# Nine loads instead of fourteen ahead of the DMA transposes of a fused dense, Mish, dense kernel

## The chip, the cores and the metric

The kernel runs on one core of one Trainium2 chip. A core has five engines with queues of their own: TensorE (PE, matmuls; its weight loads are listed apart as PEld), VectorE (DVE), ScalarE (ACT), GpSimd (POOL) and SyncE (SP). SP and ACT also issue the DMAs, each on a queue of its own; the core's 16 DMA engines carry out both queues. The metric is the time of one execution on the device in microseconds (us); the profile of one execution shows where it goes. The engines run side by side and wait for each other by semaphores only where the program says so.

## The reference

One row block `x` of 2048 x 512, two weight matrices, one bias, all bf16:

```python
B, S, D, F = 1, 2048, 512, 1792
def reference(x, w1, b1, w2):
    h = jnp.einsum("bsd,df->bsf", x, w1) + b1
    sp = jnp.log1p(jnp.exp(-jnp.abs(h))) + jnp.where(h > 0, h, jnp.zeros_like(h))
    act = h * jnp.tanh(sp)                      # Mish
    return jnp.einsum("bsf,fd->bsd", act, w2)
```

## The kernel before, in words

All of `x`, `w1` and `w2` fits into the on-chip memory, so everything is loaded once. The 2048 rows are cut into five blocks (`BLOCKS`: 256, 512, 512, 512, 256 rows). For each block, `mm1` (matmuls at line 172) computes the hidden values transposed: for each of 14 tiles f of 128 hidden columns, four matmuls (k = 0 to 3, one for each 128 of the 512 input columns) add up in one bank of PSUM. ScalarE then applies bias and Mish and writes `a_sb` in bf16 (`mish`, line 155). `mm2` (line 188) multiplies `a_sb` by `w2`: for each 128 rows, 14 matmuls of 512 columns add up in a bank, VectorE copies the result to `o_sb` (line 194), SP stores it.

`mm1` needs `x` transposed (`xT`). For blocks 1 to 4 a DMA transpose does it, issued on SP. For block 0, TensorE does it: `x_nat` holds the 256 rows as they are, `transpose_x` (line 144) transposes them through PSUM, and VectorE and ScalarE copy each half to `xT` (line 148).

The order of the work is written out by hand. Every load has a semaphore of its own (`load`, line 84), which is full only when all of the load has landed, and an instruction waits for the load that holds its operand. The loads of the start:

- on ACT's queue: the bias b1, then the k=0 rows of w1 for the first four tiles (`F0` = 4, 128 KB);
- on SP's queue: the two 128-row parts of `x_nat`; k = 1, 2, 3 of w1 for tiles 0 to 3 (128 KB each); w1 for tiles 4 to 7 in two loads (k 0 and 1, k 2 and 3, 256 KB each); w1 for tiles 8 to 13 in two (384 KB each); w2 in three (tiles 0 to 3, 4 to 8, 9 to 13: 512, 640, 640 KB); behind all of these the four DMA transposes of `x`.

TensorE's queue runs: seven dummy matmuls (`WARM`), the eight transposes of block 0, `mm1` of tiles 0 to 3 of block 0 in three passes (first 128 rows with k 0 and 1, the other 128 rows with k 0 and 1, then all 256 rows with k 2 and 3), between the second and the third of them a transpose of the bias (line 221), so that VectorE can put it into `b1_sb` (line 223) as one value per partition, which `mish` needs; then `mm1` of tiles 4 to 13 of block 0, tile after tile; `mm2` of block 0, which goes tile by tile over w2 with its two 128-row halves side by side (28 matmuls); then blocks 1 to 4, each all of `mm1` and then all of `mm2`. A PSUM bank is used again when ScalarE or VectorE has read it (`free`).

Of the kernel before, what the change touches and what calls it, by code (L numbers as in the profile page):

```python
# [4 lines left out]

P = 128
WARM = (512,) * 5 + (128,) * 2
BLOCKS = (256, 512, 512, 512, 256)


# [21 lines left out]
def bass_standalone__dense_activation_mish__prompt_kernel(  # L32
# [10 lines left out]
    BF, F32 = dt.bfloat16, dt.float32  # L43
# [3 lines left out]
    KT, FT = D // P, F // P  # L47
    assert (S, D, F) == (2048, 512, 1792) and sum(BLOCKS) == S
    x2, out2 = x[0], out[0]
# [3 lines left out]
    F0 = 4  # L53
    N0 = BLOCKS[0] // P

    with ExitStack() as es:
        def sb(name, shape, t):
            return es.enter_context(nc.sbuf_tensor(name, shape, t))

        x_nat = sb("x_nat", [P, N0, D], BF)  # L60
# [4 lines left out]
        b1_pad = sb("b1_pad", [P, P], BF)  # L65
        b1_sb = sb("b1_sb", [P, FT], F32)
        ones = sb("ones", [P, P], BF)
        ident = sb("ident", [P, P], BF)
        a_sb = sb("a_sb", [P, FT, S], BF)
        o_sb = sb("o_sb", [P, S // P, D], BF)  # L70
        ps = es.enter_context(nc.psum_tensor("ps", [P, 8, 512], F32))

        def sem(name):
            return es.enter_context(nc.semaphore(name))

        sp = Stream(nc.sync, None)
        pe = Stream(nc.tensor, sem("c_pe"))
        dve = Stream(nc.vector, sem("c_dve"))
        act = Stream(nc.scalar, sem("c_act"))
        pool = Stream(nc.gpsimd, sem("c_pool"))  # L80

        def load(q, dst, src, name, transpose=False):
            s = sem(name)
            (q.eng.dma_start_transpose if transpose else q.eng.dma_start)(dst, src).then_inc(s, 16)  # L84
            return (s, 16)

        def load_w1(q, ks, a, b):
            return load(q, w1_sb[:, ks, a * P:b * P], w1v[:, ks, a * P:b * P], "s_w1_%d_%d" % (ks.start, a))


        t_xn, t_w1 = [None] * N0, {}
        t_b1 = load(act, b1_nat[:, :], b1.rearrange("(j p) -> j p", p=P), "s_b1")
        t_xn[0] = load(sp, x_nat[:, 0, :], x2[0:P, :], "s_xn0")
        t_w1[0, 0] = load_w1(act, slice(0, 1), 0, F0)
        t_xn[1] = load(sp, x_nat[:, 1, :], x2[P:2 * P, :], "s_xn1")
        for k in range(1, KT):
            t_w1[k, 0] = load_w1(sp, slice(k, k + 1), 0, F0)
        for f in range(1, F0):
            for k in range(KT):
                t_w1[k, f] = t_w1[k, 0]  # L100
        for a, b in ((4, 8), (8, FT)):
            for ks in (slice(0, 2), slice(2, 4)):
                t = load_w1(sp, ks, a, b)
                for f in range(a, b):
                    for k in range(ks.start, ks.stop):
                        t_w1[k, f] = t
        t_w2 = {}
        for a, b in ((0, 4), (4, 9), (9, FT)):
            t = load(sp, w2_sb[:, a:b, :], w2v[:, a:b, :], "s_w2_%d" % a)
            for f in range(a, b):  # L110
                t_w2[f] = t
# [16 lines left out]
        def dummy(n):  # L128
            nc.tensor.matmul(ps[:, 7, 0:n], c_w, c_m[:, 0:n], start=True, stop=True)  # L129


        free = [[] for _ in range(8)]
# [19 lines left out]
        def mish(s, f, bank, t_mm):  # L152
            n = BLOCKS[s]
            act.wait(t_b1c, t_mm)
            t = act.mark(act.eng.activation(a_sb[:, f, starts[s]:starts[s + 1]], ps[:, bank, 0:n], ACT.Mish,  # L155
                                            bias=b1_sb[:, f:f + 1]))
            t_mish[s, f] = t
            free[bank] = [t]

        def mm1_step(s, f, k, bank, js=None):  # L160

            n = BLOCKS[s]
            lo, hi = (0, n) if js is None else (js[0] * P, (js[-1] + 1) * P)
            first = k == 0 and lo == 0
            if first:
                pe.wait(*free[bank])
            pe.wait(t_w1[k, f])
            if s:
                pe.wait(t_xT[s])
            else:  # L170
                pe.wait(*[t_cp[j, k // 2] for j in (js or range(N0))])
            return nc.tensor.matmul(ps[:, bank, lo:hi], w1_sb[:, k, f * P:(f + 1) * P],  # L172
                                    xT[:, k, starts[s] + lo:starts[s] + hi], start=first, stop=(k == KT - 1))

        def mm1(s, f, bank):
            for k in range(KT):
                mm = mm1_step(s, f, k, bank)
            mish(s, f, bank, pe.mark(mm))
# [4 lines left out]
        def mm2_step(i, f, lo, hi, bank):  # L183
            s = max(b for b in range(len(BLOCKS)) if starts[b] <= i * P)
            if f == 0:
                pe.wait(*free[bank])
            pe.wait(t_w2[f], t_mish[s, f])
            return nc.tensor.matmul(ps[:, bank, 0:hi - lo], a_sb[:, f, i * P:(i + 1) * P], w2_sb[:, f, lo:hi],  # L188
                                    start=(f == 0), stop=(f == FT - 1))
# [15 lines left out]

        for n in WARM:
            dummy(n)
        transpose_x(0)
        transpose_x(1)
        dve.wait(t_b1, t_bz)  # L210
        t_b1p = dve.mark(nc.vector.tensor_copy(b1_pad[0:FT, :], b1_nat[:, :]))  # L211
        for js, ks in (((0,), (0, 1)), ((1,), (0, 1)), ((0, 1), (2, 3))):
            for k in ks:
                for f in range(F0):
                    mm = mm1_step(0, f, k, 4 + f, js)
                    if k == KT - 1:
                        mish(0, f, 4 + f, pe.mark(mm))
            if js == (1,):
                pe.wait(t_b1p, *free[0])
                psb1 = ps[:, 0, 0:P // 2].bitcast(BF)  # L220
                t_b1t = pe.mark(nc.tensor.transpose(psb1, b1_pad[:, :], ident[:, :]))  # L221
                dve.wait(t_b1t)
                t_b1c = dve.mark(nc.vector.tensor_copy(b1_sb[:, :], psb1[:, 0:FT]))  # L223
                free[0] = [t_b1c]
        for f in range(F0, FT):
            mm1(0, f, {4: 1, 5: 2, 6: 3, 7: 0, 12: 2, 13: 3}.get(f, 4 + f % 4))
        for f in range(FT):
            for j in range(N0):
                mm = mm2_step(j, f, 0, D, j)
# [41 lines left out]
```

## Time and profile before

| what | value |
|---|---|
| time, median of 3 runs | 107.5 us (107.32 to 107.57) |
| the profiled execution | 107.65 us |
| its span, first to last instruction | 106.4 us |
| PE busy | 101.2 us (95% of the span) |
| ACT busy | 43.1 us (40%) |
| DVE busy | 12.1 us (11%) |
| loaded from HBM by plain loads / stored | 3.94 MB / 2.10 MB |

The profiled execution took 1.25 us more than its span, which lies outside of what the trace shows. A row of the timeline gives the start in us, the duration in us, the engine, the line of the kernel, the operation, what it writes and reads (the names without numbers: `w_sb` stands for both w1 and w2), the count, and in brackets how long the engine was idle before it and what ended that. SPq and ACTq are the queues of SP and ACT in which DMAs are issued: the duration there is that of the issue, not of the transfer. A row of the DMA view gives the queue, the count, the size, and the time from issue to landing. The chain of waits is followed back from the last instruction; where it names an engine, that engine worked without a break, where it names a DMA, everything waited for that DMA.

### The profile page before, as it was taken

How to read it: one execution, taken by the hardware profiler on the slowest of the kernel's cores; microseconds unless marked ns; L12 is line 12 of the kernel's file. 1: busy time of each engine (PE TensorE's matmuls, PEld its weight loads, DVE VectorE, ACT ScalarE, POOL GpSimd, SP SyncE). 2: the span in 40 equal slices, each digit the busy share in tenths (PEclk: the TensorE clock that was granted, in tenths of full speed). 3: DMA queues.
4: the chain of work that ended last, by engine and by line, in shares of the span. 5: the costliest groups of instructions: out<-in, count | busy, mean ns of one | idle time of the engine just before them, and what ended most of it. 6: DMA issues, size and time to landing. Idle time of an engine off the chain costs nothing.

```text
span 106.4 us, 1244 instructions
## 1 busy us (share of the span) xinstructions
PE 101.2 (95%) x542; PEld 51.7 (49%) x542; DVE 12.1 (11%) x22; ACT 43.1 (40%) x73; POOL 0.7 (1%) x6
## 2 busy tenths in 40 slices
PE   6957899999999999999999999999999999999993
PEld 2725754444444444444444444444444444588462
DVE  0200000400000222200000222200000222200023
ACT  2456630287772000188882000088883000199200
POOL 2000000000000000000000000000000000000000
DMA  2999999991000110110000101110000001110011
GB/s 82 259 259 312 374 244 202 208 270 66 0 0 0 49 47 8 49 49 0 0 3 0 49 12 37 55 49 0 0 0 0 28 21 49 49 55 0 0 49 49
DMA packets 13569, 7.94 MB, mean 75 GB/s; under 512 B 7932, under 2 KB 13564, under 8 KB 13564
## 3 DMA queue, kind: packets, MB, share of 16 engines
q1 hardware_dynamic: 13392, 7.74, 27.4%
q10 hardware_dynamic: 172, 0.13, 0.4%
q8 instruction: 4, 0.07, 0.3%
q14 instruction: 1, 0.01, 0.0%
HBM read 3.94 MB, written 2.10 MB: 57 GB/s over the span
## 4 chain that ended last, share of the span: by engine, by line
PE 88%; DMA 6%; SPq 3%; issue 0%; DVE 0%
PE ps L188 45%; PE ps L172 42%; DMA w_sb<-in_w_dram 6%; SPq L84 3%; DVE o_sb L194 0%
## 5 line engine op out<-in xcount | busy, mean ns | idle before, releaser
L155 ACT ACTIVATE a_sb<-ps,b_sb 128x512 bf16<-128x512 f32 (+1 forms) x70 | 41.0, 602 | 53.4 <-PE ps L172 53.4
L172 PE MATMUL ps<-xT,w_sb 128*128 128x512 bf16 (+2 forms) x288 | 50.2, 332 | 2.5 <-DMA w_sb<-in_w_dram 1.9
L188 PE MATMUL ps<-w_sb,a_sb 128*128 128x512 bf16 (+2 forms) x238 | 49.2, 366 | 0.0
L172 PEld LDWEIGHTS ps<-xT,w_sb 128*128 128x128 bf16 x288 | 27.2, 98 | 25.0 <-DMA w_sb<-in_w_dram 3.0
L188 PEld LDWEIGHTS ps<-w_sb,a_sb 128*128 128x128 bf16 x238 | 22.8, 98 | 25.5
L194 DVE CAST o_sb<-ps 128x512 bf16<-128x512 f32 (+2 forms) x17 | 11.1, 659 | 88.0 <-PE ps L188 88.0
L129 PE MATMUL ps<-const-bfloat16-1.0 128*128 128x512 bf16 (+1 forms) x7 | 2.5, 533 | 0.8 <-PEq L256 0.8
L123 ACT ACT_TABLE_LOAD x1 | 1.3, 1283 | 1.9 <-issue 1.9
L129 PEld LDWEIGHTS ps<-const-bfloat16-1.0 128*128 128x128 bf16 x7 | 0.9, 135 | 2.2 <-issue 2.2
L148 ACT ACTIVATE xT<-ps 128x256 bf16<-128x256 bf16 x2 | 0.8, 383 | 0.6 <-PE ps L144 0.6
L144 PE MATMUL ps<-ident,x_nat 128*128 128x128 bf16 x8 | 1.0, 305 | 0.0
L148 DVE COPY xT<-ps 128x256 bf16<-128x256 bf16 x2 | 0.6, 292 | 2.7 <-PE ps L144 2.6
L144 PEld LDWEIGHTS ps<-ident,x_nat 128*128 128x128 bf16 x8 | 0.9, 147 | 0.0
L223 DVE CAST b_sb<-ps 128x14 f32<-128x14 bf16 x1 | 0.2, 173 | 1.1 <-PE ps L221 1.1
L121 POOL TENSOR_SCALAR_AFFINE_SELECT ident<-ones 128x128 bf16<-128x128 bf16 x1 | 0.3, 292 | 0.1
L221 PE MATMUL ps<-ident,b_pad 128*128 128x128 bf16 x1 | 0.2, 219 | 0.0
L118 DVE MEMSET b_pad<- 128x64 uint32 x1 | 0.1, 112 | 0.9 <-PEq L256 0.9
L119 POOL MEMSET ones<- 128x128 bf16 x1 | 0.2, 204 | 0.3 <-POOLq L256 0.3
L211 DVE COPY b_pad<-b_nat 14x128 bf16<-14x128 bf16 x1 | 0.2, 172 | 0.0
L256 POOL MEMSET const-bfloat16-1.0<- 128x1 bf16 x1 | 0.1, 101 | 0.0
L256 POOL MEMSET const-uint8-127<- 128x1 uint8 x1 | 0.1, 101 | 0.0
L256 POOL MEMSET const-float32-0.0<- 128x1 f32 x1 | 0.1, 98 | 0.3 <-issue 0.3
(2 smaller groups left out, 0.2 us busy)
## 6 DMA issues: line engine op xcount, KB each, us to landing
out_dram<-o_sb SPq DMA_DIRECT2D x15, 128.0 KB, 1.7
w_sb<-in_w_dram SPq DMA_DIRECT2D x2, 640.0 KB, 9.4
w_sb<-in_w_dram SPq DMA_DIRECT2D x2, 384.0 KB, 6.3
w_sb<-in_w_dram SPq DMA_DIRECT2D x2, 256.0 KB, 4.3
w_sb<-in_w_dram SPq DMA_DIRECT2D x1, 512.0 KB, 7.5
w_sb<-in_w_dram SPq DMA_DIRECT2D x3, 128.0 KB, 2.9
x_nat<-in_x_dram SPq DMA_DIRECT2D x2, 128.0 KB, 2.0
w_sb<-in_w_dram ACTq DMA_DIRECT2D x1, 128.0 KB, 2.5
```

Source lines behind the costliest of these rows:

```text
L84: (q.eng.dma_start_transpose if transpose else q.eng.dma_start)(dst, src).then_inc(s, 16)
L119: t_ones = pool.mark(pool.eng.memset(ones[:, :], 1.0))
L121: t_id = pool.mark(pool.eng.affine_select(ident[:, :], ones[:, :], pattern=[[1, P]], compare_op=ALU.is_equal, fill=0.0, base=0, channel_mu ...
L123: act.eng.preload_act_table(ACT.Mish)
L129: nc.tensor.matmul(ps[:, 7, 0:n], c_w, c_m[:, 0:n], start=True, stop=True)
L144: mm = nc.tensor.transpose(psb[:, i * P:(i + 1) * P], x_nat[:, j, k * P:(k + 1) * P], ident[:, :])
L148: t = eng.mark(nc.vector.tensor_copy(dst, src) if eng is dve else act.eng.activation(dst, src, ACT.Copy))
L155: t = act.mark(act.eng.activation(a_sb[:, f, starts[s]:starts[s + 1]], ps[:, bank, 0:n], ACT.Mish, bias=b1_sb[:, f:f + 1]))
L172: return nc.tensor.matmul(ps[:, bank, lo:hi], w1_sb[:, k, f * P:(f + 1) * P], xT[:, k, starts[s] + lo:starts[s] + hi], start=first, stop=( ...
L188: return nc.tensor.matmul(ps[:, bank, 0:hi - lo], a_sb[:, f, i * P:(i + 1) * P], w2_sb[:, f, lo:hi], start=(f == 0), stop=(f == FT - 1))
L194: t = dve.mark(nc.vector.tensor_copy(o_sb[:, i, lo:hi], ps[:, bank, 0:hi - lo]))
L256: nc = _bacc.Bacc("TRN2", target_bir_lowering=False, num_devices=1)
```

## The change

The loads ahead of the DMA transposes are cut into fewer pieces and dealt out otherwise to the two queues. w1 of tiles 0 to 3 goes in two loads of 256 KB (k 0 and 1; k 2 and 3), both on ACT's queue and first there; b1 is third on ACT's queue. SP's queue has the two parts of `x_nat`, then w1 of tiles 4 to 7 in one load (512 KB), w1 of tiles 8 to 13 in one (768 KB), w2 in two (tiles 0 to 4: 640 KB, tiles 5 to 13: 1152 KB), then the four DMA transposes as before. These are 9 loads where there were 14 (8 and 13 without b1).

The transpose of the bias moves behind the `mm1` of tile 4, and with it the five `mish` of tiles 0 to 4, which are issued on ScalarE's queue after VectorE has put the bias in place. Tile 4 has bank 1 as before. The dummy matmuls are six of 512 columns instead of five of 512 and two of 128.

```diff
-WARM = (512,) * 5 + (128,) * 2
+WARM = (512,) * 6
...
-        t_xn, t_w1 = [None] * N0, {}
+        t_xn, t_w1, t_w2 = [None] * N0, {}, {}
+        for ks in (slice(0, 2), slice(2, 4)):
+            t = load_w1(act, ks, 0, F0)
+            for f in range(F0):
+                for k in range(ks.start, ks.stop):
+                    t_w1[k, f] = t
+        for j in range(N0):
+            t_xn[j] = load(sp, x_nat[:, j, :], x2[j * P:(j + 1) * P, :], "s_xn%d" % j)
         t_b1 = load(act, b1_nat[:, :], b1.rearrange("(j p) -> j p", p=P), "s_b1")
-        t_xn[0] = load(sp, x_nat[:, 0, :], x2[0:P, :], "s_xn0")
-        t_w1[0, 0] = load_w1(act, slice(0, 1), 0, F0)
-        t_xn[1] = load(sp, x_nat[:, 1, :], x2[P:2 * P, :], "s_xn1")
-        for k in range(1, KT):
-            t_w1[k, 0] = load_w1(sp, slice(k, k + 1), 0, F0)
-        for f in range(1, F0):
-            for k in range(KT):
-                t_w1[k, f] = t_w1[k, 0]
         for a, b in ((4, 8), (8, FT)):
-            for ks in (slice(0, 2), slice(2, 4)):
-                t = load_w1(sp, ks, a, b)
-                for f in range(a, b):
-                    for k in range(ks.start, ks.stop):
-                        t_w1[k, f] = t
-        t_w2 = {}
-        for a, b in ((0, 4), (4, 9), (9, FT)):
+            t = load_w1(sp, slice(0, KT), a, b)
+            for f in range(a, b):
+                for k in range(KT):
+                    t_w1[k, f] = t
+        for a, b in ((0, 5), (5, FT)):
             t = load(sp, w2_sb[:, a:b, :], w2v[:, a:b, :], "s_w2_%d" % a)
...
+        done = []
         for js, ks in (((0,), (0, 1)), ((1,), (0, 1)), ((0, 1), (2, 3))):
             for k in ks:
                 for f in range(F0):
                     mm = mm1_step(0, f, k, 4 + f, js)
                     if k == KT - 1:
-                        mish(0, f, 4 + f, pe.mark(mm))
-            if js == (1,):
-                pe.wait(t_b1p, *free[0])
-                psb1 = ps[:, 0, 0:P // 2].bitcast(BF)
-                t_b1t = pe.mark(nc.tensor.transpose(psb1, b1_pad[:, :], ident[:, :]))
-                dve.wait(t_b1t)
-                t_b1c = dve.mark(nc.vector.tensor_copy(b1_sb[:, :], psb1[:, 0:FT]))
-                free[0] = [t_b1c]
-        for f in range(F0, FT):
-            mm1(0, f, {4: 1, 5: 2, 6: 3, 7: 0, 12: 2, 13: 3}.get(f, 4 + f % 4))
+                        done.append((f, 4 + f, pe.mark(mm)))
+        for k in range(KT):
+            mm = mm1_step(0, F0, k, 1)
+        done.append((F0, 1, pe.mark(mm)))
+        pe.wait(t_b1p, *free[0])
+        psb1 = ps[:, 0, 0:P // 2].bitcast(BF)
+        t_b1t = pe.mark(nc.tensor.transpose(psb1, b1_pad[:, :], ident[:, :]))
+        dve.wait(t_b1t)
+        t_b1c = dve.mark(nc.vector.tensor_copy(b1_sb[:, :], psb1[:, 0:FT]))
+        free[0] = [t_b1c]
+        for f, bank, t in done:
+            mish(0, f, bank, t)
+        for f in range(F0 + 1, FT):
+            mm1(0, f, {5: 2, 6: 3, 7: 0, 12: 2, 13: 3}.get(f, 4 + f % 4))
```

## The prediction

> **What bounds the kernel now.** I read the page first, then the chain of waits, then TensorE's rows of the first 20 us, then where each load landed. In the page, the groups of TensorE:
>
> ```profile
> span 106.4 us, 1244 instructions
> L172 PE MATMUL ps<-xT,w_sb 128*128 128x512 bf16 (+2 forms) x288 | 50.2, 332 | 2.5 <-DMA w_sb<-in_w_dram 1.9
> L188 PE MATMUL ps<-w_sb,a_sb 128*128 128x512 bf16 (+2 forms) x238 | 49.2, 366 | 0.0
> ```
>
> TensorE is the bound, and all that it idles once it has begun is some 2.5 us in line 172, nearly all for loads. The chain says where:
>
> ```profile
> 4.64 6.50 DMA w_sb<-in_w_dram
> 11.15 0.05 issue
> 11.19 2.58 PE ps L172 x22
> 13.77 6.04 PE ps L188 x28
> 19.81 12.09 PE ps L172 x56
> 104.56 0.29 DVE o_sb L194
> ```
>
> From 11.19 us to the end TensorE never waits. What came last ahead of it is one load, issued at 4.64: k 2 and 3 of w1's tiles 8 to 13. So the time is the moment when TensorE gets its last needed operand in block 0, plus a fixed rest, and I have to find that moment in the changed kernel. TensorE's rows:
>
> ```profile
> 0.84 2.50 PE L129 MATMUL ps<-const-bfloat16-1.0 128*128 128x512 bf16 x7 [0.84 <-PEq L256]
> 3.14 1.01 PE L144 MATMUL ps<-ident,x_nat 128*128 128x128 bf16 x8
> ...
> 5.26 0.22 PE L221 MATMUL ps<-ident,b_pad 128*128 128x128 bf16 x1
> 5.31 1.04 PE L172 MATMUL ps<-xT,w_sb 128*128 128x256 bf16 x8
> 7.38 0.39 PE L172 MATMUL ps<-xT,w_sb 128*128 128x256 bf16 x2 [1.03 <-DMA w_sb<-in_w_dram]
> 8.07 1.70 PE L172 MATMUL ps<-xT,w_sb 128*128 128x256 bf16 x14 [0.30 <-DMA w_sb<-in_w_dram]
> 10.29 0.38 PE L172 MATMUL ps<-xT,w_sb 128*128 128x256 bf16 x2 [0.52 <-ACT a_sb L155]
> 11.19 2.58 PE L172 MATMUL ps<-xT,w_sb 128*128 128x256 bf16 x22 [0.52 <-DMA w_sb<-in_w_dram]
> 13.61 6.21 PE L188 MATMUL ps<-w_sb,a_sb 128*128 128x512 bf16 x28
> 19.65 0.59 PE L172 MATMUL ps<-xT,w_sb 128*128 128x512 bf16 x2
> ```
>
> The pairs at 7.38 and 10.29 are what split loads buy: each pair (k 0 and 1 of one tile) runs while the other half of the load is still under way. From the starts: 22 matmuls of 256 columns in 13.61 - 11.19 = 2.42 us, 0.110 each; 28 of 512 columns in 19.65 - 13.61 = 6.04 us, 0.216 each.
>
> Which loads are close behind? The issue on SP's queue, and below it the time to landing of the same DMAs in the same order (the load of 256 KB; the last two of w2; the first DMA transpose):
>
> ```profile
> 3.62 0.47 SPq L84 DMA_DIRECT2D w_sb<-in_w_dram  x1
> 5.68 0.55 SPq L84 DMA_DIRECT2D w_sb<-in_w_dram  x1
> 6.27 1.09 SPq L84 DMA_DIRECT2D w_sb<-in_w_dram  x1
> 7.40 8.60 SPq L84 DMA_TRANSPOSE xT<-in_x_dram  x1
> ```
>
> ```profile
> w_sb<-in_w_dram SPq DMA_DIRECT2D x1, 256.0 KB, 4.4
> w_sb<-in_w_dram SPq DMA_DIRECT2D x1, 640.0 KB, 8.8
> w_sb<-in_w_dram SPq DMA_DIRECT2D x1, 640.0 KB, 9.9
> xT<-in_x_dram SPq DMA_TRANSPOSE x1, 12.1
> ```
>
> Landings: w1 of tiles 4 to 7 complete at 8.0, w2 of tiles 4 to 8 at 14.5, w2 of tiles 9 to 13 at 16.2, the first transpose at 19.5. Needed: w2's tile 4 at 13.61 + 8 x 0.216 = 15.3, its tile 9 at 13.61 + 18 x 0.216 = 17.5, the first transpose at 19.65. So w2 has 0.8 and 1.3 us to spare, the transpose 0.15. What the DMA engines move (the last figure of a row; the last but one is their busy share):
>
> ```profile
> 2.00:5.50 3.50, 3.40 (x32) 2.44 (x31) 0.67 (x3) 1.94 (x3) 0.00 (x0) 1.00 0.91 265
> 5.50:8.00 2.50, 1.24 (x10) 0.61 (x8) 0.17 (x1) 1.57 (x4) 0.00 (x0) 1.00 0.93 260
> 8.00:10.50 2.50, 1.91 (x16) 1.42 (x16) 0.00 (x0) 1.78 (x4) 0.00 (x0) 1.00 0.91 308
> 10.50:14.00 3.50, 2.98 (x26) 2.37 (x25) 0.00 (x0) 2.38 (x6) 0.00 (x0) 1.00 1.09 370
> ```
>
> They are busy throughout, at 260 to 308 GB/s on x and w1 and at 370 on w2.
>
> **The change part by part.** I call S the time by which the stream of loads is ahead of now, and first set S = 0: the bytes ahead of each point are the same in both kernels (x and w1's tiles 0 to 3, then 4 to 7, then 8 to 13, then w2), so a merged load lands when its last part lands now.
>
> *w1 of tiles 8 to 13 in one load.* It lands when the load at 4.64 does, and TensorE starts at 11.19 with 24 matmuls in place of 22, as the pair at 10.29 has lost its early half: 11.19 + 24 x 0.110 = 13.83 for the start of mm2, +0.22 us.
>
> *w1 of tiles 4 to 7 in one load.* The pair at 7.38 moves behind 8.07: 16 x 0.110 = 1.76 and the bias transpose (0.05, from its start to the next) end at 9.9. Hidden: the next load comes at 11.19. The cover is 1.3 us.
>
> *w2 in two loads.* Tiles 0 to 4 land 128 KB beyond the present first load, well before 14.5, where the present second lands with all 640 KB; at 370 GB/s some 0.35 us after 12.7 (5.16 + 7.5), near 13.0, and they are needed at 13.83: hidden. Tiles 5 to 13 hang on one semaphore that is full at 6.27 + 9.9 = 16.17, now needed from tile 5 on, at 13.83 + 10 x 0.216 = 15.99. Here is a new wait, 0.2 us: 18 matmuls are left at 16.2, 3.88 us, so mm2 of block 0 ends at 20.09 instead of 19.65. The two terms together: +0.44 us.
>
> ```profile
> w_sb<-in_w_dram SPq DMA_DIRECT2D x1, 512.0 KB, 7.5
> 5.16 0.48 SPq L84 DMA_DIRECT2D w_sb<-in_w_dram  x1
> ```
>
> *What the stream gains, S.* Six issues leave SP's queue: three of w1's tiles 0 to 3, which ACT's takes over in two loads where it had one, and one each by the merging of tiles 4 to 7, of 8 to 13 and of w2:
>
> ```profile
> 2.19 0.43 SPq L84 DMA_DIRECT2D w_sb<-in_w_dram  x1
> 2.66 0.43 SPq L84 DMA_DIRECT2D w_sb<-in_w_dram  x1
> 0.80 0.67 ACTq L84 DMA_DIRECT2D b_nat<-in_b_dram  x1
> 1.49 0.36 ACTq L84 DMA_DIRECT2D w_sb<-in_w_dram  x1
> ```
>
> One 128 KB issue each 0.47 us is 279 GB/s, hardly above the 265 that flowed up to 5.5 us, so the issue may have paced the stream there. Against that stands 5.5 to 8.0 us: SP was then over 1 MB ahead with loads twice as large, and the engines moved 260 all the same. So S from below is 0 by that row; two queues that mix on the same engines could cost something (the nearest row is the same 260 against 265: 2% of the first 3.5 us, -0.1). From above: if 2.0 to 5.5 us ran at the 308 of the next row but one, it would save 3.5 x (1 - 265/308) = 0.5 us. I take S = 0.2, nearer the backlogged row. Both terms move one for one with S, so the end is +0.44 - 0.2 = +0.24 us.
>
> The Trainium skill ("DMA: Bandwidth & Descriptors", Issuing engines are not separate DMA queues) says that queues on several engines share the same 16 DMA engines and save only issue time. By that sentence S is at most what the issue had held back; the row of 260 GB/s under a full backlog would make that nothing, and the sum +0.44.
>
> *The bias third on ACT, its transpose and five Mish later.* b1 is behind 512 KB that ACT's queue shares with SP's: 768 KB of x and w1 by 265 GB/s from 2.0 are there near 5 to 6 us, and the bias is wanted behind tile 4's matmuls, 8.07 + 4 x 0.11 = 8.5. Cover 2 us. The transpose, the copy and then the Mish rows:
>
> ```profile
> 5.51 0.17 DVE L223 CAST b_sb<-ps 128x14 f32<-128x14 bf16 x1 [1.11 <-PE ps L221]
> 8.50 1.78 ACT L155 ACTIVATE a_sb<-ps,b_sb 128x256 bf16<-128x256 f32 x4 [0.81 <-PE ps L172]
> ```
>
> b1_sb is ready near 8.9; at 0.435 each the five end at 11.1 and tile 7's at 12.4. Bank 4 is wanted by tile 8 at 11.19 and is free after the first (9.4); bank 0 by mm2 at 13.8. Free, with 1.4 us of cover; beyond that each late 0.1 us costs 0.1.
>
> *The dummies.* 2816 columns now take 2.30 us, 6 x 512 take 2.51: the transposes start at 3.35 instead of 3.14, and x_nat's second part shares the engines with w1's first load, so that it lands near 4.0 (512 KB at 265 GB/s from 2.0). All of it is ahead of the wait for w1's tiles 4 to 7, where TensorE idles over 1 us now: nothing. More dummies and the same gaps leave the clock as it is (128 to 256 columns at 0.43 ns a column after 5.3 us).
>
> *The transposes.* SP issues the first sooner, but the issue lasted 8.60 us, to 16.00, since it stands behind the loads: it lands at 19.5 - S for a need at 19.89. Not on the path.
>
> **Sum.** 107.65 us, the profiled execution, +0.24 = 107.89. That execution was 0.15 above the median, so 107.74 for the median: +0.2%, just at the limit. About 0.2% (0.21 us) is what a measurement of this kernel can tell from no change.
>
> **Rivals.**
> 1. *Faster: the early stream is denser.* With two loads in flight from 0.8 us and no gap between small loads, S is 0.75: w1 of tiles 8 to 13 at 10.44, mm2 at 13.08, tile 5 wanted at 15.24, w2 there at 15.45, end 19.33, that is -0.32: 107.2. It decides from S = 0.44 on. For: a busy share of 0.91 leaves 9%. Against: the row at 260.
> 2. *Much faster: large loads run at w2's rate.* If it is the size of the load and not the place of w1's rows in HBM that makes 260 against 370, then 5.5 to 10.5 us shrink: 2.5 x 260/370 + 2.5 x 308/370 = 3.84 us, S = 1.16, end -0.72: 106.8 (with the first 3.5 us too, S = 2.1 and 105.8). Against: from 128 KB to 256 KB the rate did not rise. The Trainium skill ("DMA: Bandwidth & Descriptors", Bandwidth, Measured) has this as a rule: batch to 1 MiB for 75% of peak, 138 GB/s at 64 KB and 341 at 1 MB. The trace agrees for w2's loads, and not between the first two rows.
> 3. *Slower still: the merged loads land late.* Mixed queues put x and w1 behind each other and hold up the slowest DMA engine by 0.5 us: S = -0.5, +0.94: 108.4. For: the slice from 4.5 to 5 us moved far less than its neighbours:
>
> ```profile
> 4.50:5.00 0.50, 0.42 (x8) 0.43 (x9) 0.00 (x0) 0.07 (x1) 0.00 (x0) 1.00 0.89 213
> ```
>
> 4. *The change does nothing:* S happens to cancel 0.44 within 0.2 us: inside my own range.
>
> **How the numbers follow.** Forecast (S from -0.1 to 0.5: 107.45 to 108.05): 0.50, of it slower by over 0.2% 0.36 and within it 0.14. Rival 1: 0.22, of it faster 0.16, within 0.06. Rival 2: 0.14, faster. Rival 3: 0.14, slower. Together faster 0.30, same 0.20, slower 0.50. The range from 106.5 to 108.4 leaves out the far halves of rivals 2 and 3.
>
> **What would show it.** Right: a wait of TensorE in line 185 (mm2) for `w_sb` near 16 us; 24 matmuls behind the wait for w1's tiles 8 to 13, and that wait ending near 11.0; the same 260 GB/s up to 8 us. Wrong: that wait ends before 10.7, or mm2 of block 0 runs without a break; 300 GB/s and more up to 8 us; a wait for a Mish (the bias came late) or for the first transpose ahead of block 1.

## The result and the profile after

The changed kernel takes 106.46 us (median of 4 runs, 106.33 to 106.62) beside 107.41 (107.19 to 107.57) for the kernel before: a ratio of 0.9913 with a 95% interval of 0.9889 to 0.9937. It is faster by 0.95 us where 0.24 us slower was forecast, and 0.04 us below the lower end of the range. Below, a time is the median of all runs of a kernel, with their range, while a ratio to the kernel before, measured again beside it, goes by the runs within 1.5% of each kernel's fastest.

The profiled execution took 106.62 us. Its page, the span and TensorE's two groups:

```profile
span 105.4 us, 1227 instructions
L169 PE MATMUL ps<-xT,w_sb 128*128 128x512 bf16 (+2 forms) x285 | 50.0, 334 | 0.7 <-DMA w_sb<-in_w_dram 0.3
L185 PE MATMUL ps<-w_sb,a_sb 128*128 128x512 bf16 (+2 forms) x232 | 48.7, 366 | 0.4
```

TensorE's idle time in `mm1` (line 169 now) has fallen from 2.5 to 0.7 us, and `mm2` (line 185), which waited for nothing before, idles 0.4 us. (A few matmul records are missing in this trace: 285 and 232 of the 288 and 238.) The chain of waits of the changed kernel, where it leaves the loads:

```profile
3.29 11.41 DMA w_sb<-in_w_dram
14.70 0.05 issue
14.74 4.06 PE ps L185 x18
18.80 4.75 PE ps L169 x22
```

The last thing that everything waits for is now the second load of w2, issued at 3.29 and landed at 14.70; the 18 matmuls of tiles 5 to 13 follow it. TensorE's rows of the changed kernel:

```profile
3.35 0.63 PE L141 MATMUL ps<-ident,x_nat 128*128 128x128 bf16 x4
4.42 0.61 PE L141 MATMUL ps<-ident,x_nat 128*128 128x128 bf16 x4 [0.44 <-DMA x_nat<-in_x_dram]
4.82 2.38 PE L169 MATMUL ps<-xT,w_sb 128*128 128x128 bf16 x24
7.52 0.61 PE L169 MATMUL ps<-xT,w_sb 128*128 128x256 bf16 x4 [0.32 <-DMA w_sb<-in_w_dram]
...
9.72 2.78 PE L169 MATMUL ps<-xT,w_sb 128*128 128x256 bf16 x24 [0.23 <-ACT a_sb L152]
12.55 6.25 PE L185 MATMUL ps<-w_sb,a_sb 128*128 128x512 bf16 x27
18.64 1.67 PE L169 MATMUL ps<-xT,w_sb 128*128 128x512 bf16 x7
```

Tiles 8 to 13 start at 9.72 instead of 11.19, block 1 at 18.64 instead of 19.65: that second difference, 1.01 us, is the gain in the span (106.4 to 105.4). (The wait at 9.72 is put down to ScalarE, which came last by this trace; the load for the same matmuls, issued at 2.19, landed at 9.6. The first of the 28 matmuls of mm2 is one of the missing records: 24 x 0.109 after 9.72 is 12.34.) And what the DMA engines moved:

```profile
2.00:5.50 3.50, 3.06 (x19) 1.77 (x18) 0.58 (x2) 2.05 (x3) 0.00 (x0) 1.00 0.96 324
5.50:8.00 2.50, 2.18 (x25) 1.79 (x24) 0.18 (x1) 0.00 (x0) 0.00 (x0) 1.00 1.06 369
8.00:10.50 2.50, 2.27 (x23) 1.83 (x21) 0.17 (x1) 2.07 (x6) 0.00 (x0) 1.00 1.10 358
```

Where the kernel before moved 265, 260 and 308 GB/s, this one moves 324, 369 and 358. That is 0.21 + 0.27 + 0.13 = 0.6 MB more by 10.5 us, or 1.6 us of loading at 370 GB/s. The gain is a faster stream of loads; the experiments ask which part of the edit makes it so.

### The profile page after: what moved, and what is told of

It is laid out like the page before. It is cut to its first block, busy times and chain, and to the rows that moved or that the text cites. A ratio compares the mean times of both kernels' runs of the same rounds, so it can differ in the third digit from the quotient of the medians.

```text
span 105.4 us, 1227 instructions
## 1 busy us (share of the span) xinstructions
PE 101.1 (96%) x532; PEld 52.0 (49%) x541; DVE 12.2 (12%) x22; ACT 42.3 (40%) x73; POOL 0.7 (1%) x6
## 4 chain that ended last, share of the span: by engine, by line
PE 84%; DMA 11%; SPq 2%; issue 1%; DVE 0%
PE ps L185 44%; PE ps L169 40%; DMA w_sb<-in_w_dram 11%; SPq L84 2%; DVE o_sb L191 0%
## 5 line engine op out<-in xcount | busy, mean ns | idle before, releaser
L152 ACT ACTIVATE a_sb<-ps,b_sb 128x512 bf16<-128x512 f32 (+1 forms) x70 | 40.2, 611 | 52.2 <-PE ps L169 49.3
L185 PE MATMUL ps<-w_sb,a_sb 128*128 128x512 bf16 (+2 forms) x232 | 48.7, 366 | 0.4
L169 PEld LDWEIGHTS ps<-xT,w_sb 128*128 128x128 bf16 x288 | 27.8, 100 | 22.2 <-DMA w_sb<-in_w_dram 0.6
L126 PE MATMUL ps<-const-bfloat16-1.0 128*128 128x512 bf16 x6 | 2.7, 623 | 0.8 <-PEq L258 0.8
## 6 DMA issues: line engine op xcount, KB each, us to landing
w_sb<-in_w_dram SPq DMA_DIRECT2D x1, 1152.0 KB, 11.4
```

## The experiments

The theories at the start: the rate follows the size and number of the loads (size), it follows how the stream begins (start), or it is low as long as SP issues (issue). Two numbers tell them apart better than the time does: the rates in the three stretches above, and when the last load of w2 lands (16.2 us before, 14.7 after). Each is from one trace. How far they can be trusted is told by traces of the same loads: w2 lands at 16.2 and 16.5 us in two with the loads of the kernel before, at 14.7, 14.3 and 14.3 in three with those of the changed kernel, at 14.7 and 14.5 in two with the changed start alone (these kernels follow below). The kernel before ran again beside each group: median 107.62, 107.44, 107.66 and 107.78 us.

**Later loads merged alone.** The kernel before with

```diff
-            for ks in (slice(0, 2), slice(2, 4)):
-                t = load_w1(sp, ks, a, b)
+            t = load_w1(sp, slice(0, KT), a, b)
...
-        for a, b in ((0, 4), (4, 9), (9, FT)):
+        for a, b in ((0, 5), (5, FT)):
```

> The kernel before, with only the later loads merged: w1 of tiles 4 to 7 in one load, of tiles 8 to 13 in one, w2 in two; the first loads (x, w1 of tiles 0 to 3 in four pieces of 128 KB, b1 first) and the order of the work as before. Size theory (the rate follows the size and the number of the loads): w1 of tiles 4 to 13 flows at 350 GB/s and more instead of 260 to 308, the last load of w2 lands 1.0 to 1.4 us sooner than 16.2, time 106.5 to 106.9. Start theory (two queues busy from the first loads on): the rate up to 10.5 us stays at 260 to 310, S is 0, and the two new waits cost 0.44: 107.85. Issue theory (the stream is slow as long as SP issues loads): SP's issue ends near 5.9 instead of 7.4, S is 0.4 to 0.7, time 107.1 to 107.4.

Measured: 109.42 us (108.62 to 109.74), 1.4% slower than before (interval of the ratio 1.0079 to 1.0194), outside of what any theory gave. The rates are 218, 342 and 378 GB/s, and w2 is complete at 17.0. So merging does raise the rate of the later loads behind the old first loads, but the early stretch is worse than before, and w2 lands later. And something happens to TensorE that no theory had: stretches of this kernel (the figure before the last two is the granted clock), and its matmuls of tiles 4 to 13:

```profile
6.20:9.50 3.30, 1.01 (x8) 0.42 (x6) 0.09 (x1) 1.57 (x4) 0.00 (x0) 1.00 1.02 373
9.60:12.90 3.30, 3.01 (x15) 2.16 (x16) 0.00 (x0) 1.18 (x3) 0.00 (x0) 0.50 1.10 353
13.00:15.60 2.60, 2.60 (x26) 2.33 (x25) 0.00 (x0) 2.42 (x7) 0.00 (x0) 1.00 1.76 220
```

```profile
9.89 6.02 PE L171 MATMUL ps<-xT,w_sb 128*128 128x256 bf16 x40 [2.38 <-DMA w_sb<-in_w_dram]
```

TensorE waited 2.4 us for the merged load of tiles 4 to 7; the clock was then granted at half for the whole of the 3.3 us shown, in which 15 matmuls ran where the next 2.6 us held 26. This is a second mechanism beside the stream: a wait early on costs twice when it lets the clock fall.

**The start alone.** The changed kernel with the later loads cut as before (the diff above, reversed; five of w1 and w2's tiles 4 to 13 become seven again).

> The changed kernel with the later loads cut as before: w1 of tiles 4 to 7 in two, of tiles 8 to 13 in two, w2 in three; w1 of tiles 0 to 3 stays in two loads on ACT's queue, b1 third. Size theory: only the first four pieces are larger, S is 0.2 to 0.4, time 107.0 to 107.2. Start theory: S is 1.0 to 1.5 as in the changed kernel, w1's last load lands near 9.7 to 10.1, time 106.3 to 106.6. Issue theory: SP's issue ends near 5.9, S is 0.4 to 0.7, time 106.7 to 107.0.

Measured: 106.44 us (105.74 to 106.92), ratio 0.9852 (0.9786 to 0.9917). Its stretches, and a row of TensorE for later:

```profile
2.00:5.50 3.50, 2.90 (x16) 1.46 (x15) 0.58 (x2) 1.84 (x3) 0.00 (x0) 1.00 1.05 310
5.50:8.00 2.50, 2.50 (x21) 2.19 (x19) 0.18 (x1) 0.21 (x1) 0.00 (x0) 1.00 1.03 366
8.00:10.50 2.50, 2.50 (x24) 2.17 (x23) 0.17 (x1) 1.21 (x4) 0.00 (x0) 1.00 1.09 361
```

```profile
5.08 3.91 PE L170 MATMUL ps<-xT,w_sb 128*128 128x128 bf16 x28
```

w2 is complete at 14.7, as in the changed kernel. In the stretches where the loads of 256 and 384 KB moved at 260 and 308 in the kernel before, they move at 366 and 361 here. So the later loads need not be large to be fast, against the size theory, and the stream is not slow as long as SP issues (here until 5.7 us, at 310), against the issue theory. The new first loads alone give the whole gain of the stream; merging the later ones adds nothing to it.

**The order of the work alone.** The loads of the kernel before with the changed kernel's dummies, bias and Mish order.

> The loads of the kernel before, with the changed kernel's order of the work: six dummy matmuls, the bias transpose behind tile 4 and the five Mish after it. All three theories of the stream: landings as before (w1's last load near 11.1), so within 0.15 us of before. If the later Mish or the longer warm-up were what moves the time: a difference of more than 0.3 us with unchanged landings.

Measured: 107.85 us (107.03 to 108.53), ratio 1.0003 (0.9966 to 1.0040); 253, 277 and 248 GB/s, w2 complete at 16.5. With the old loads the order is worth nothing that can be measured.

**b1 first.** The changed kernel with the load of b1 moved ahead of w1 on ACT's queue.

> The changed kernel with b1 first on ACT's queue instead of third. If the small first load is what held the stream up in the kernel before (an issue of 0.67 us in front of w1, rows of 256 B): the rate up to 8 us falls back towards 260 and the time to 107 and more. By the size, start and issue theories the loads of w1 on ACT's queue start 0.7 us later and the time stays within 0.3 us of the changed kernel: 106.4 to 106.8.

Measured: 107.92 us (106.76 to 110.64). The stream comes out between the two predictions: 254 GB/s up to 5.5, then 381 and 358, w2 complete at 15.1, against 14.3 to 14.7 with b1 third. The time is worse than that, and the spread wide: in the trace, which is of one of the longer runs (109.71), TensorE waited three times for loads between 4 and 8 us, and its 256-column matmuls ran at half pace to 12.8 (23 in the 4.7 us from 8.1, 27 in the 2.7 us from 12.9). b1 third is worth 0.4 to 0.8 us of the stream; that the rest of the time comes from the gaps that it spares TensorE is read from this one trace.

Now what it is in the first loads: ACT's queue or their size.

**Four loads on ACT's queue.**

```diff
-        for ks in (slice(0, 2), slice(2, 4)):
+        for ks in [slice(k, k + 1) for k in range(KT)]:
             t = load_w1(act, ks, 0, F0)
```

> The changed kernel with w1 of tiles 0 to 3 cut into four loads of 128 KB, all four still on ACT's queue, b1 behind them (fifth). Queue theory (what matters is that these loads stand on ACT's queue, so that two queues feed the DMA engines from the start): the stream as in the changed kernel, w1's last load near 9.6 us, w2's last near 14.7, time 106.3 to 106.8. Piece theory (pieces of 128 KB are what held the stream up): 2.0 to 5.5 us falls back to 220 to 270 GB/s, w1's last load lands at 10.6 to 11.2, w2's last at 15.7 or later, time 107.4 or more.

**Two loads on SP's queue**, behind x:

```diff
+        for j in range(N0): t_xn[j] = load(sp, ...)
         for ks in (slice(0, 2), slice(2, 4)):
-            t = load_w1(act, ks, 0, F0)
+            t = load_w1(sp, ks, 0, F0)
```

> The changed kernel with the two loads of w1's tiles 0 to 3 (256 KB each) on SP's queue behind x, so that ACT's queue has b1 alone. Queue theory: one queue feeds the engines, 2.0 to 5.5 us at 220 to 270 GB/s, w1's last load 10.5 or later, time 107.2 or more. Piece theory: the stream as in the changed kernel to within 0.4 us (the issue of two more loads on SP), time 106.3 to 106.9.

The stretches, first of the four loads on ACT's queue, then of the two on SP's:

```profile
2.00:5.50 3.50, 3.33 (x28) 1.77 (x26) 0.58 (x2) 1.94 (x3) 0.00 (x0) 1.00 0.88 255
5.50:8.00 2.50, 0.06 (x1) 0.07 (x2) 0.00 (x0) 0.00 (x0) 0.00 (x0) 0.85 1.02 331
```

```profile
2.00:5.50 3.50, 2.43 (x13) 1.22 (x12) 0.67 (x3) 1.53 (x3) 0.00 (x0) 1.00 0.85 250
5.50:8.00 2.50, 1.92 (x24) 1.57 (x24) 0.00 (x0) 0.00 (x0) 0.00 (x0) 1.00 0.97 317
```

Measured: 110.43 us (108.78 to 111.28) with w2 complete at 16.2, and 108.21 (107.60 to 109.64) with w2 at 16.4. Neither theory alone holds: the four on ACT's queue fail the queue theory, the two on SP's the piece theory. It takes both, large pieces and the second queue, as far as one trace each can tell (that of the four loads is of a run of 110.47). Of the first kernel's time much is the clock again (TensorE ran one matmul from 5.5 to 8.0, and was granted 0.5 from 8.0 to 10.5).

**The same edit in the kernel before.** There w1 of tiles 0 to 3 goes in two loads on ACT's queue behind b1; all else is as before.

> The kernel before with one edit: w1 of tiles 0 to 3 goes in two loads of 256 KB on ACT's queue behind b1 (b1 stays first, the later loads stay cut as they were, the order of the work too). If the first loads alone carry the gain of the stream, w2's last load lands near 15.1 (as with b1 first in the changed kernel) instead of 16.2, w1's last near 9.9 instead of 11.1, and the time is 106.3 to 106.9 where TensorE's clock comes up in time, up to 108 where it does not. If it takes the merging of the later loads as well: landings within 0.3 us of before, time 107.3 to 107.8.

Measured: the landings as expected by the first reading, w1's last at 10.1 and w2's at 15.3 (265, 378 and 366 GB/s). The time is 107.74, from 105.74 to 108.59: with b1 first and the bias transpose early, TensorE waits 2.3 us for w1 near 4.2 to 6.5, and in the trace (a run of 108.56) its clock is at 0.50 from 8.0 to 11.4. Two of its ten runs took 105.74 and 106.39, the others 107.66 to 108.59; that the two are those in which the clock came up in time is likely, but no trace shows it.

**Split again, and a bridge.** The start of the changed kernel, the later loads cut as before, and

```diff
         transpose_x(0)
+        for n in (512, 128):
+            dummy(n)
         transpose_x(1)
```

> The changed kernel with the later loads cut as before (as in the run with the start only) and two more dummy matmuls (512 and 128 columns) between the two halves of the TensorE transposes, where TensorE waited 0.8 us for x. Clock theory (TensorE's matmuls run at half rate until it has been busy for a whole period of about 3.4 us, and a gap early on puts that off): the 256-column matmuls reach 0.11 us each by 6 us at the latest, the spread of the runs is under 0.6 us, and with w1's last load at 9.4 and 22 matmuls behind it the time is 105.5 to 105.9. If the gaps do not matter for the clock: as without the dummies, 105.7 to 106.9.

Measured: 105.87 us (105.57 to 106.12), ratio 0.9854 (0.9813 to 0.9894). The spread is 0.55 us and the time inside the range of the clock theory, but it is inside that of the other reading too. TensorE's rows:

```profile
3.83 0.74 PE L127 MATMUL ps<-const-bfloat16-1.0 128*128 128x512 bf16 x2
4.52 0.61 PE L142 MATMUL ps<-ident,x_nat 128*128 128x128 bf16 x4
4.92 3.13 PE L170 MATMUL ps<-xT,w_sb 128*128 128x128 bf16 x28
7.89 0.22 PE L224 MATMUL ps<-ident,b_pad 128*128 128x128 bf16 x1
7.94 4.09 PE L170 MATMUL ps<-xT,w_sb 128*128 128x256 bf16 x36
12.09 5.99 PE L186 MATMUL ps<-w_sb,a_sb 128*128 128x512 bf16 x27
17.92 1.46 PE L170 MATMUL ps<-xT,w_sb 128*128 128x512 bf16 x6
```

From 4.52 on TensorE waits for no load at all. The 28 matmuls, 3.13 us here, took 3.91 in the run with the start alone, which has no bridge, and none of them waited there either: half pace lasted longer in that trace, behind a gap of 0.60 us. A gap doesn't always do that: behind one of 0.48 us they took 2.63 us in the second trace of the changed kernel (below). All runs of this kernel lie below all runs of the changed one. Over the start alone no gain is shown but the narrower spread: the ratios, 0.9854 and 0.9852, are the same.

**The bridge in the changed kernel alone.**

> The changed kernel with the two dummy matmuls between the halves of the TensorE transposes alone (the later loads stay merged). The waits for w1's tiles 8 to 13 (landing near 9.6, 24 matmuls behind it) and for w2's second load (14.7) are still there, so mm2 of block 0 ends near 18.6 as before the bridge: 106.2 to 106.5, with a spread under 0.5 us. If the bridge alone, and not the splitting, made the run with both fast: 105.7 to 106.0.

Measured: 106.16 us (106.06 to 106.20), ratio 0.9874 (0.9837 to 0.9911), between the two expectations. The 28 matmuls took 2.69 us, but w2's second load still held tile 5 up, to 14.33, and block 1 started at 18.23, against 17.92 with the loads cut again. The bridge is worth 0.3 us here, as all four runs lie below all five of the unaltered kernel on the same chip (106.22 to 106.73, below). No trace shows where, since the one of the unaltered kernel is of its fastest run, with block 1 at 18.25. What the cutting adds is shown by these 0.3 us between the traces alone; the ratios (0.9854 and 0.9874) don't tell the two apart.

**Three variations of the start.** The queues exchanged (w1 first on SP's, x on ACT's); one load of 512 KB on ACT's queue; the changed kernel once more.

> The changed kernel with the queues of the first loads exchanged: the two 256 KB loads of w1's tiles 0 to 3 first on SP's queue, the two parts of x first on ACT's, b1 third there. If it takes two queues and two large first loads, whichever queue has which: 2.0 to 5.5 us at 310 GB/s and more, w2's last load at 14.5 to 15.2 (SP has two issues more ahead of the rest). If it takes ACT's queue for w1: w2's last load at 16 or later, time 107.4 or more.

> The changed kernel with w1 of tiles 0 to 3 in one load of 512 KB on ACT's queue instead of two of 256 KB. If larger first loads are what keeps the stream smooth: w2's last load at 14.4 to 14.8 as in the changed kernel. TensorE gets k 0 and 1 later (near 5.0 instead of 4.0 us), so it has a longer gap early on: 106.4 to 107.5 by how TensorE's clock takes that. If two loads of 256 KB just happened to suit: w2's last load at 15.7 or later.

> The changed kernel once more, unaltered, on the chip of this comparison: w2's last load at 14.4 to 15.0 as in its first trace, time 106.3 to 106.7, ratio to before 0.985 to 0.994. If the smooth stream of the first trace was luck: a landing of 15.5 or later, or a spread of over 1 us.

Measured: exchanged, 107.11 us (106.15 to 107.79), 298, 354 and 366 GB/s, w2 at 15.6: nearly the rates of the changed kernel, so it isn't ACT's queue as such, but the last load gains only 0.6 us of 1.5, and lands 0.4 us beyond what was expected. One load: 302, 376 and 353 GB/s, w2 at 14.2, as expected, with 107.88 us (106.21 to 108.38). In its trace (108.11) TensorE's first longer gap, 1.4 us, is for the second part of x, which lands at 5.4, behind k 0 and 1 at 5.0; three of its ten runs took 106.2 to 106.5. The repetition: 106.44 us (106.22 to 106.73), ratio 0.9912 (0.9878 to 0.9946), w2 at 14.3.

**Why the first loads act on later ones.** One queue with w1 first; and the kernel before with one load more, first on ACT's queue, of 256 bytes of each of w1's rows, beside a control that takes them from w2:

```diff
+        load(act, extra[:, :, :], w1v[:, :, 0:P], "s_extra")         # w2v[:, 0:KT, 0:P] in the control
         t_b1 = load(act, b1_nat[:, :], ...)
```

> The changed kernel with the two 256 KB loads of w1's tiles 0 to 3 first on SP's queue, x behind them on the same queue, b1 alone on ACT's. If it takes two queues that both hold large loads from the start: the stream as in the run with both on SP behind x, 2.0 to 8.0 us at 250 to 320 GB/s, w2's last load at 16 or later. If it is enough that w1 is read in large loads before anything small: w2's last load at 14.3 to 15.3. x comes behind 512 KB, near 4 to 4.5 us, so the time by itself says less than the landings.

> The kernel before with one load more, first on ACT's queue: the first 256 bytes of each of w1's 512 rows (128 KB, into a buffer that nothing reads); everything else as before. First-access theory (the first reads of w1's rows are slow, 0.3 to 0.9 us each, and when they come in small doses they put the 16 DMA engines out of step): behind this load w1 flows at 320 GB/s and more and w2's last load lands at 15.5 or sooner in spite of 128 KB more. Otherwise: 16.2 plus the 0.5 us of the added load, 16.5 to 17.

> The same with the added load taken from w2 (the first 256 bytes of 512 of its rows) instead of w1. First-access theory: w1's rows stay cold, the stream is slow, w2's last load at 16.5 to 17. If the added load helped only because it is a large first load on the second queue, whatever it reads: w2's last load at 15.5 or sooner here too.

Measured: one queue, 108.76 us (108.24 to 109.79), 224, 333 and 363 GB/s, w2 at 16.3: large loads of w1 ahead of everything are not enough on one queue. The two added loads, w1 and then the control, in the stretch from 5.5 to 8.0:

```profile
5.50:8.00 2.50, 1.66 (x16) 1.66 (x17) 0.00 (x0) 0.00 (x0) 0.00 (x0) 1.00 1.06 360
5.50:8.00 2.50, 1.48 (x15) 1.48 (x16) 0.00 (x0) 0.00 (x0) 0.00 (x0) 1.00 0.85 273
```

After touching w1's rows the small loads of w1 move at 360 GB/s, after touching w2's at 273, as without (one trace each). That half of the first-access theory came true; the other did not: w2 was complete at 16.1, not 15.5 (16.7 in the control), as the first stretch sank to 232 and 219. The times are 108.17 (107.27 to 109.53), not told apart from before (ratio 1.0023, 0.9983 to 1.0064), and 108.28 (107.72 to 109.68), a little worse (1.0052, 1.0011 to 1.0093).

The traces also hold a record of every DMA packet. From 5.5 to 10.5 us a packet of 1 KB takes 0.046 to 0.051 us in the median, in slow and fast streams alike, but a few packets of w1 and w2 take 0.2 to 2.2 us. In the kernel before they are 24 and take 10.8 us together, of the 80 that 16 engines have in 5 us; with the order alone 36 and in the control 17, after touching w1's rows 7, in the two traces of the changed kernel 3 and none. So part of what a slow stream loses is lost in a few held-up packets. The packets of the touch itself were not among them: none of its 512 took over 0.018 us.

All kernels together (GB/s in the three stretches; us). The kernels ran on several chips, so that times of different rows are best compared by the ratio:

| kernel | 2.0-5.5 | 5.5-8.0 | 8.0-10.5 | w2 complete | time | ratio |
|---|---|---|---|---|---|---|
| before | 265 | 260 | 308 | 16.2 | 107.41 | 1 |
| order alone | 253 | 277 | 248 | 16.5 | 107.85 | 1.0003 |
| touch w2 (control) | 219 | 273 | 310 | 16.7 | 108.28 | 1.0052 |
| touch w1 | 232 | 360 | 373 | 16.1 | 108.17 | 1.0023 |
| later loads merged | 218 | 342 | 378 | 17.0 | 109.42 | 1.0137 |
| two on SP behind x | 250 | 317 | 341 | 16.4 | 108.21 | 1.0066 |
| two on SP, w1 first | 224 | 333 | 363 | 16.3 | 108.76 | 1.0108 |
| four on ACT | 255 | 331 | 379 | 16.2 | 110.43 | 1.0201 |
| two on ACT, b1 first | 254 | 381 | 358 | 15.1 | 107.92 | 0.9990 |
| the same in before | 265 | 378 | 366 | 15.3 | 107.74 | 0.9863 (2 of 10 runs) |
| queues exchanged | 298 | 354 | 366 | 15.6 | 107.11 | 0.9942 |
| one on ACT | 302 | 376 | 353 | 14.2 | 107.88 | 0.9936 (5 of 10 runs) |
| changed (first, second trace) | 324, 301 | 369, 365 | 358, 352 | 14.7, 14.3 | 106.46, 106.44 | 0.9913, 0.9912 |
| changed with the bridge | 307 | 364 | 353 | 14.3 | 106.16 | 0.9874 |
| start alone | 310 | 366 | 361 | 14.7 | 106.44 | 0.9852 |
| start alone with the bridge | 317 | 366 | 359 | 14.5 | 105.87 | 0.9854 |

Two regularities stand out. The first stretch reaches some 300 only where w1 and x stand first on two different queues, w1 in pieces of 256 KB or more. The second and third stretch are low only where w1's tiles 0 to 3 came in 128 KB pieces, the later loads were cut too, and nothing else had read w1's rows.

## Why the prediction was wrong, step by step

- **S, what the stream gains: the step that failed.** It was taken as 0.2 us with 0.5 as the upper end; it is 16.17 - 14.70 = 1.47 at w2's last load and 11.14 - 9.6 = 1.5 at w1's. The reason given, that 260 GB/s under a full backlog was what the engines can do with such loads, fell: loads cut the same way moved at 366 in the run with the start alone. The 260 was the outcome of how the stream had begun. The upper end came from the row of 308; by the row of 370, in the same view, the first stretch alone could give 1.0 and all three 2.1 us.
- **The rest of the sum held.** With S put in as measured, 1.47, it gives 20.09 - 1.47 = 18.62 for the end of mm2 in block 0, and block 1 starts at 18.64; the time, 107.65 + 0.44 - 1.47 = 106.62, is that of the profiled run.
- **24 matmuls behind the merged load**: right, in one row at 9.72.
- **The new wait for w2's second load**: right. Tile 5 was wanted at 12.34 + 10 x 0.216 = 14.50 and came at 14.74, 0.24 us late where 0.2 was worked out. Cutting that load again, as in the run with split loads and bridge, removes it.
- **The bias**: hidden as said. The first Mish starts at 8.43 instead of 6.12, and TensorE waits for none beyond the 0.2 us noted at 9.72, when the load had only just landed.
- **The dummies and x**: x_nat's second part landed at 4.4 (near 4.0 was said), a gap of 0.44 us. In the first trace it cost nothing, as TensorE waited 0.3 us for w1 later anyhow. That the gaps leave the clock as it is held in this kernel's traces, but not in those of its neighbours: with merged loads, four loads, and two loads in the kernel before, waits of 2.3 to 2.5 us were followed by a clock of 0.50. The Trainium skill ("TensorE: Matmul & The Clock Gate", Part 1: The HAM clock gate) says that the clock comes up after some 3.4 us of sustained work and goes to half after an idle window of that length. The trace with merged loads agrees with the length, with 0.50 from 9.6 to 12.9; but the wait ahead of it was only 2.4 us, in a stretch of 3.3 us in which TensorE was also busy for 1.0.
- **The transposes**: right. SP issued the first at 4.04, but the issue lasted to 14.5; it landed at 18.0 and was wanted at 18.64.
- **The rivals.** Rival 2 had the size of the gain nearly (106.8 at S = 1.16, 105.8 at 2.1), but not its cause: the later loads need not be large, as the start alone shows. The rule behind it is to batch towards 1 MiB (the Trainium skill, "DMA: Bandwidth & Descriptors", Bandwidth), and its figures are for loads issued from GpSimd, where these are issued from SP and ACT. It isn't needed here: loads of 256 and 384 KB moved at 361 to 366 GB/s behind the new first loads, and merging them gained nothing more. Rival 1 had one place, the early stream. Of the 1.6 us of loading that were gained by 10.5 us some 0.6 lie ahead of 5.5, where rival 1 put its 0.75, and 1.1 behind it, where rival 2 put 1.16: each had a part.
- **The rule on queues.** By the Trainium skill ("DMA: Bandwidth & Descriptors", Issuing engines are not separate DMA queues) a second queue saves only issue time. Two loads on SP's queue instead of ACT's cost 1.7 us of the stream (16.4 against 14.7), where their two issues are worth 1.0 us; the measurement goes beyond the rule, by more than the 0.4 us between traces of the same loads.

## What to carry to other kernels

A transfer rate under a full backlog was here the rate of that order of loads, not of the engines: when a change reorders the first loads, bound its gain by the best row of the same view. At the start of a kernel, try the first operands in pieces of 256 KB or more at the head of two queues at once, small loads behind them, and later loads cut where a first part is wanted early. Keep TensorE busy through early waits: ones of 2.3 to 2.5 us were followed by half the clock for over 3 us in four traces here (one of 2.05 was not).

## What was not expected of the hardware

How the first microseconds of loading go sets the rate for the next five: 260 against 366 GB/s for loads cut the same way, depending on what came ahead of them. One load that only touches w1's rows brought it from 273 to 360. That first accesses to w1's rows are slow, and disturb the loads least when they come all at once on two queues, would fit the rates, but it is not shown: the touch did not mend the first stretch, its own 512 first reads took 0.018 us at most, and w2, whose rows were as new, moved at 370 in the kernel before. What holds single packets up, and why two loads of 256 KB on a second queue do, and four of 128 KB do not, stays open.
